# Score bursts of a causal attention block: two tiles in one bank, no splitting, and the mask written by VectorE

## The chip, the cores and the metric

One core of a Trainium2 chip runs the whole program. The metric is the device time of one execution in microseconds (us). The kernel before takes 1286.41 us as the median of three runs (1285.4 to 1286.81).

## The reference

Block-causal attention over 8 batches and 8 heads (576 positions, head size 64, blocks of 64 positions), followed by a two-layer network with a rational activation over all 4608 tokens:

```python
scores = scale * np.matmul(q, k.transpose(0, 1, 3, 2))          # 8 x 8 x 576 x 576
mask = (pos[:, None] // 64) >= (pos[None, :] // 64)
scores = np.where(mask, scores, -1000000000.0)
attn = softmax(scores)                                            # row maximum subtracted
x = (attn @ v) as 4608 x 512
h = x @ w_in                                                      # 512 -> 2048
g = (a0 + a1*h + a2*h^2 + a3*h^3) / (1 + |b0|*|h| + |b1|*h^2 + 1e-6)
out = g @ w_out                                                   # 2048 -> 512
```

## The kernel before

**Attention.** Heads are worked on in 32 pairs (`p` = 0 to 31, two heads each, called h = 0 and 1). `load` fetches q and k of a pair, `prep` transposes them on TensorE (PE) and splits each value into a rounded high part and a rest, so that a product is three matmul passes (high x high, high x low, low x high). A pair has five query tiles, taken in the order `TILES = (4, 3, 2, 0, 1)` (index `d`): tiles 0 to 3 are 128 query rows wide and see 128*(i+1) keys; tile 4 holds the last 64 rows of both heads and all 576 keys.

**Scores.** `scores(p, d, j)` emits the matmuls of one tile. For tiles 0 to 3 one head's contraction has only 64 rows, so head 0 uses the upper 64 rows of the PE array and head 1 the lower 64; matmuls of the two heads alternate, each head into a PSUM bank of its own, and `behind` keeps their order. In what follows such a group is called a burst, and its form shows in the profile as `64*128` (all other matmuls are `128*128`). In tiles 0 to 3 the last 64 keys of the first 64 rows are forbidden. Before, a matmul of the constant tiles `mrow` and `mcol` (line 504) adds -2^30 there, ahead of the three passes (line 507): two mask matmuls and six score matmuls per burst, in four bursts per pair.

**Softmax and the rest.** VectorE (DVE) reads each bank for the row maximum (line 518, tile `nm`), ScalarE (ACT) reads it for the exponential with its sum (`expo`, line 529), GpSimd (POOL) scales (line 541), PE transposes the probabilities (`transp`, line 567), ACT and DVE split them in high and low (580, 581), and PE multiplies with v (`pv`, lines 617 and 633). The results go through DRAM (`xscr`) to the network.

**The network.** Class `Ffn` works in units: `first` is the matmuls of line 210, then an activation spread over ACT, POOL and DVE, then `second` with the matmuls of line 277. Ten of sixteen column groups of the hidden layer are done while attention runs (phase 0), the other six after it (phase 1). Which unit is emitted beside which attention step is set by a table of due steps (`there`, `goal`).

**What sets the order.** Each engine works its own queue strictly in the order of the built program; waits between engines are semaphores. That order comes from a scheduler that runs the emitted program against its own model of times, honouring data dependencies and the extra edges made by `behind`. PSUM has 8 banks: five are the pool `ps_a` (tag `a`) of attention, from which scores, transposes and v products take one bank each in turn; one is `ps_h`, two are `ps_o`, of the network.

Of the kernel before, what the change touches and what calls it, by code (L numbers as in the profile page):

```python
# [8 lines left out]
F32 = mybir.dt.float32  # L9
F32R = mybir.dt.float32r  # L10
I32 = mybir.dt.int32
U32 = mybir.dt.uint32
AF = mybir.ActivationFunctionType
ALU = mybir.AluOpType
AX = mybir.AxisListType
# [10 lines left out]
LEND = 4  # L26
RL = 3
C0 = 0
RW = 4
EV = 6  # L30
DP = 12
# [24 lines left out]
NEG = -float(2 ** 30)  # L56
TILES = (4, 3, 2, 0, 1)
PH, PK = 30, 7
MASKS = ((None, None), (0, 0), (0, 1), (1, 0))
QC = 1.0 + 1e-6  # L60

WSCALE = 2.0 ** -112
# [3 lines left out]
def attn_ffn_kernel(  # L66
# [11 lines left out]
    nc = tc.nc  # L78
# [30 lines left out]
    class Weights:  # L109
# [22 lines left out]
        def convert(self):  # L132
            last = []
            for key in self.places:
# [8 lines left out]
                                        in_=src.bitcast(I32).rearrange("(d p) f -> p d f", p=128))  # L143
                if there and len(last) >= RW:
                    tc.add_manual_dep(got.ins, last[-RW].ins.name,
                                      mybir.DependencyInfo(mybir.DependencyClass.Sync, mybir.DependencyReason.DATA),
# [26 lines left out]
    class Ffn:  # L173
# [8 lines left out]
        def load(self, ph, c):  # L182
            n = CTS[ph]
            nd = 512 // n
            self.x[ph, c] = []
            for i in range(4 // nd):

                pool = self.pools[-1] if ph and (4 * c + i) % 6 < 3 else ffn
                x = pool.tile([128, nd, 2, n], F32R, name=f"x{ph}_{c}_{i}", tag="x", bufs=XB)
                t0 = c * n  # L190
                while t0 < (c + 1) * n:
                    b = t0 // S
                    t1 = min((c + 1) * n, (b + 1) * S)
                    for d in range(nd):
                        nc.sync.dma_start(out=x[:, d, :, t0 - c * n:t1 - c * n].bitcast(F32),
                                          in_=xscr[b][:, nd * i + d, :, t0 - b * S:t1 - b * S])
                    t0 = t1
                self.x[ph, c] += [x[:, d] for d in range(nd)]
# [135 lines left out]
    with ExitStack() as actx:  # L334
        ps_a = actx.enter_context(tc.tile_pool(name="ps_a", bufs=5, space=PSUM))
        att = actx.enter_context(tc.tile_pool(name="att", bufs=2))
        apers = actx.enter_context(tc.tile_pool(name="apers", bufs=1))
# [4 lines left out]
        pts.append(apers.tile([128, 640], F32, name="p4"))  # L342
        vz = apers.tile([128, 5, 2, 128], F32, name="vz", tag="v")
        vst = []
        mrow = apers.tile([128, 128], F32R, name="mrow")
        mcol = apers.tile([128, 64], F32R, name="mcol")
        for x in qtl:
            nc.gpsimd.memset(x.bitcast(F32), 0.0)
        nc.gpsimd.memset(mrow.bitcast(F32), 0.0)
        nc.gpsimd.memset(mcol.bitcast(F32), NEG)  # L350
        for r in (0, 64):
            nc.gpsimd.memset(mrow[r:r + 1, 0:64].bitcast(F32), 1.0)
        nc.gpsimd.memset(pts[4][:, S:], 0.0)
        nc.gpsimd.memset(vz, 0.0)

# [46 lines left out]
        def behind(ins, first):  # L402
            tc.add_manual_dep(ins.ins, first.ins.name,
                              mybir.DependencyInfo(mybir.DependencyClass.NoSync, mybir.DependencyReason.DATA),
                              reason="order")
# [74 lines left out]
        def scores(p, d, j):  # L480
            s = st_[p]
            if j == 0:
                s[d] = tuple(att.tile([128, 2], F32, name=f"{n}{p}_{d}", tag=n, bufs=4) for n in ("nm", "sm"))
            nm, sm = s[d]
            i = TILES[d]
            q, k = s["q"], s["k"]
            if i == 4:
                c0, w = 288 * j, 288
                ps = ps_a.tile([128, 512], F32, name=f"s{p}_{d}_{j}", tag="a")
                for n, (x, y) in enumerate(((0, 0), (0, 1), (1, 0))):  # L490
                    nc.tensor.matmul(ps[:, :w], lhsT=qtl[p % 2][:, x], rhs=k[:, y, c0:c0 + w],  # L491
                                     start=(n == 0), stop=(n == 2))
                s[d, j] = ps
            else:
                w = 128 * (i + 1)
                if j == 0:
                    for h in range(2):
                        s[d, h] = ps_a.tile([128, 512], F32, name=f"s{p}_{d}_{h}", tag="a")
                    prev = None
                    for n, (x, y) in enumerate(MASKS):  # L500
                        for h in (1, 0):
                            hs = slice(64 * h, 64 * h + 64)
                            if x is None:
                                mm = nc.tensor.matmul(s[d, h][:, w - 64:w], lhsT=mrow[hs], rhs=mcol[hs],  # L504
                                                      start=(n == 0), stop=(n == 3), skip_group_check=(n == 0))
                            else:
                                mm = nc.tensor.matmul(s[d, h][:, :w], lhsT=q[hs, x, 128 * i:128 * i + 128],  # L507
                                                      rhs=k[hs, y, 0:w], start=(n == 0), stop=(n == 3),
                                                      skip_group_check=(MASKS[0][0] is None))
                            if prev is not None:  # L510
                                behind(mm, prev)
                            prev = mm
            if i == 4 and j == 1:
                nc.vector.tensor_tensor_reduce(out=trash, in0=s[d, j][:, :w], in1=zero.to_broadcast([128, 288]),
                                               scale=-1.0, scalar=nm[:, 0:1], op0=ALU.add, op1=ALU.min,
                                               accum_out=nm[:, 0:1])
            else:
                nc.vector.reduce_max(out=nm[:, j:j + 1], in_=s[d, j][:, :w], axis=AX.X, negate=True)  # L518

        def expo(p, d, j):  # L520
            s = st_[p]
            nm, sm = s[d]
            i = TILES[d]
            if i == 4 and j == 0:
                return
            for j2 in (0, 1) if i == 4 else (j,):
                n, w = (0, 288) if i == 4 else (j2, 128 * (i + 1))
                dst = pts[4][:, 288 * j2:288 * j2 + 288] if i == 4 else pts[i][:, j2]
                nc.scalar.activation(out=dst, in_=s.pop((d, j2))[:, :w], func=AF.Exp,  # L529
                                     bias=nm[:, n:n + 1], scale=1.0, accum_out=sm[:, j2:j2 + 1])  # L530
            if j == 0:
                return
            rc = att.tile([128, 2], F32, name=f"rc{p}_{d}", tag="rc", bufs=4)
            n = 1 if i == 4 else 2
            if i == 4:
                nc.gpsimd.tensor_tensor(out=sm[:, 0:1], in0=sm[:, 0:1], in1=sm[:, 1:2], op=ALU.add)
            nc.gpsimd.tensor_scalar_add(rc[:, :n], sm[:, :n], 1e-9)
            nc.vector.reciprocal(rc[:, :n], rc[:, :n])  # L538
            for j2 in range(n):
                x = pts[4][:, 0:S] if i == 4 else pts[i][:, j2]  # L540
                nc.gpsimd.tensor_scalar(out=x, in0=x, scalar1=rc[:, j2:j2 + 1], scalar2=1.0,  # L541
                                        op0=ALU.mult, op1=ALU.mult)
# [102 lines left out]
        def attn_steps():  # L645
# [8 lines left out]
            for k in range(len(items) + ALAG2 + ALAG3 + 8):  # L654
                for x in [x for x in todo if x[0] == k]:
                    todo.remove(x)
                    x[1](*x[2])
                if k < len(items):
                    p, d, j = items[k]
                    if (d, j) == (0, 0):  # L660
                        if p + 1 < NV:
                            o0, o1, o2 = OFFS
                            at(k + o0, load, p + 1)
                            at(k + o1, prep, p + 1, 0)
                            at(k + o2, prep, p + 1, 1)
                    at(k + ALAG2, expo, p, d, j)
                    if j == 1:
                        at(k + TLAG, transp, p, d)
                        if d == 4:
                            at(k + TLAG + 1, pv, p, 0)  # L670
                            at(k + TLAG + 2, pv, p, 1)
                            if p + 1 < NV:
                                at(k + TLAG + 2, vprep, p + 1)
                    scores(p, d, j)
                yield k
# [4 lines left out]
        load(0)  # L680
        for _ in range(C0):
            next(wsteps)
# [18 lines left out]
        NWA, NWB = 2 * NFA, 2 * NFB  # L701
        wdone = C0
        WSTEPS = [0] * C0 + [(W0 * (i + 1)) // 4 for i in range(4 - C0)] + [WA + WD * i // 4 for i in range(NWA - 4)]

# [56 lines left out]
```

## Time and profile before

| what | value |
|---|---|
| median of three runs | 1286.41 us |
| profiled execution | 1287.04 us |
| its span, first to last instruction | 1285.3 us |
| granted PE clock | 0.998 of full |
| busy: PE, DVE, ACT, POOL | 1255.0, 904.0, 925.3, 880.5 us |
| mask matmuls (line 504) | 256, at 9.8 to 834.8 us |
| score matmuls (line 507) | 768, at 10.0 to 835.3 us |

Times are in us from the span's start. PE matmuls overlap each other, so the busy time of PE is more than what its matmuls stream; the distance from one matmul's start to the next one's start is what a matmul costs the queue. The last scores stand at 835 us: what comes after is the network alone.

### The profile page before, as it was taken

The numbers are of one execution on the slowest core, as the hardware profiler recorded it, in microseconds if no ns is written. First come the engines' busy times: TensorE is split into PE (matmuls) and PEld (weight loads), VectorE is DVE, ScalarE is ACT, GpSimd is POOL, SyncE is SP. The second block draws the span as 40 slices with busy tenths as digits, with TensorE's granted clock in tenths as the row PEclk, the third lists the DMA queues.
The fourth block names the chain that finished last, engine by engine and source line by source line (L and its number), as shares of the span: only waits on it lengthen the run. The fifth ranks groups of instructions, "written<-read, shape, count | busy, mean of one in ns | idle before, by whom it ended". The sixth has DMA issues, their size and how long they took to land.

```text
span 1285.3 us, 22748 instructions
## 1 busy us (share of the span) xinstructions
PE 1255.0 (98%) x7644; PEld 1059.5 (82%) x7644; DVE 904.0 (70%) x1703; ACT 925.3 (72%) x2047; POOL 880.5 (69%) x1041
## 2 busy tenths in 40 slices
PE   7989999999999999999999999999999999999997
PEld 5667888888888888888888888888998888888886
DVE  5767678777777777777767676754666767666675
ACT  5878777788678788777878787866766565555553
POOL 4656677777777878777767676766777666666564
PEclk9999999999999999999999999999999999999999
DMA  8772253445444354443432432356111433333423
GB/s 223 210 213 74 71 170 89 131 109 144 107 121 123 114 140 112 131 126 82 135 91 74 114 93 67 89 175 232 50 49 50 131 98 125 125 129 130 155 75 107
DMA packets 206516, 153.81 MB, mean 120 GB/s; under 512 B 137792, under 2 KB 170560, under 8 KB 206400
## 3 DMA queue, kind: packets, MB, share of 16 engines
q1 hardware_dynamic: 203920, 151.77, 40.5%
q8 instruction: 61, 1.00, 0.3%
q10 hardware_dynamic: 2416, 0.59, 0.2%
q14 instruction: 55, 0.45, 0.1%
q0 software_dynamic: 64, 0.00, 0.0%
HBM read 98.57 MB, written 44.04 MB: 111 GB/s over the span
## 4 chain that ended last, share of the span: by engine, by line
PE 82%; ACT 7%; DVE 4%; DMA 3%; POOL 3%; issue 1%; SPq 0%; ACTq 0%; POOLq 0%; DVEq 0%
PE h L210 30%; PE o L277 28%; PE o L633 6%; PE t L567 5%; PE s L507 4%; PE s L504 3%; ACT p L529 2%; PE tp L416 2%; PE s L491 1%; PE o L594 1%; DMA x<-xscr 1%; PE o L617 1%; DMA xscr<-xl 1%; POOL u L244 1%; ACT s L219 1%
## 5 line engine op out<-in xcount | busy, mean ns | idle before, releaser
L210 PE MATMUL h<-x,wpi 128*128 128x256 f32 (+1 forms) x2808 | 462.8, 312 | 3.1 <-DMA x<-xscr 1.7
L210 PEld LDWEIGHTS h<-x,wpi 128*128 128x128 f32 x2808 | 396.4, 190 | 40.6 <-issue 4.0
L277 PE MATMUL o<-wpo,gh 128*128 128x512 f32 x1152 | 351.0, 397 | 1.3 <-ACT os L287 1.3
L277 PEld LDWEIGHTS o<-wpo,gh 128*128 128x128 f32 x1152 | 211.1, 188 | 43.7 <-ACT os L287 1.8
L277 PE MATMUL o<-wpo,gl 128*128 128x512 f32 x576 | 213.8, 401 | 1.2 <-POOL gl L256 1.1
L224 POOL TENSOR_TENSOR u<-v,u 128x512 f32<-128x512 f32 x144 | 186.7, 1297 | 29.7 <-ACT v L220 24.6
L541 POOL TENSOR_SCALAR p<-p,rc 128x128 f32<-128x128 f32 (+4 forms) x288 | 169.2, 599 | 48.0 <-DVE rc L538 40.3
L529 ACT ACTIVATE p<-s,nm 128x288 f32<-128x288 f32 (+4 forms) x320 | 167.8, 533 | 45.1 <-DVE nm L518 39.9
L225 DVE TENSOR_TENSOR s<-s,h 128x512 f32<-128x512 f32 x144 | 98.4, 683 | 110.4 <-ACT s L219 56.7
L244 POOL TENSOR_TENSOR u<-s,u 128x512 f32<-128x512 f32 x90 | 116.7, 1297 | 72.1 <-DVE u L242 58.1
L232 ACT ACTIVATE v<-u,qcb 128x512 f32<-128x512 f32 x144 | 105.1, 730 | 74.7 <-POOL u L224 74.3
L217 ACT ACTIVATE u<-h 128x512 f32<-128x512 f32 x144 | 86.0, 597 | 93.7 <-PE h L210 87.9
L518 DVE TENSOR_REDUCE nm<-s 128x1 f32<-128x128 f32 (+4 forms) x288 | 128.5, 477 | 23.8 <-PE s L507 16.2
L567 PE MATMUL t<-ident,p 128*128 128x128 f32 x800 | 126.5, 281 | 0.9 <-POOL u L224 0.4
L581 DVE TENSOR_TENSOR ptrl<-t,ptrh 128x512 fp32r<-128x512 f32 (+1 forms) x182 | 111.6, 627 | 18.9 <-ACT ptrh L580 17.4
L277 PEld LDWEIGHTS o<-wpo,gl 128*128 128x128 f32 x576 | 104.3, 189 | 23.5 <-POOL gl L256 3.3
L256 POOL TENSOR_TENSOR gl<-u,v 128x512 fp32r<-128x512 f32 x90 | 118.6, 1317 | 3.4
L259 POOL TENSOR_TENSOR gl<-s,gh 128x512 fp32r<-128x512 f32 x54 | 69.9, 1294 | 62.9 <-ACT gh L258 62.9
L567 PEld LDWEIGHTS t<-ident,p 128*128 128x128 f32 x800 | 92.8, 142 | 23.1 <-issue 8.1
L580 ACT CAST ptrh<-t 128x512 fp32r<-128x512 f32 (+1 forms) x182 | 95.7, 545 | 18.8 <-PE t L567 18.2
L226 DVE SCALAR_TENSOR_TENSOR s<-s,coef,h 128x512 f32<-128x512 f32 x144 | 107.2, 744 | 2.9
L507 PE MATMUL s<-k,q 64*128 64x512 f32 (+3 forms) x768 | 103.5, 351 | 0.0
(109 smaller groups left out, 2105.6 us busy)
## 6 DMA issues: line engine op xcount, KB each, us to landing
x<-xscr SPq DMA_DIRECT2D x56, 256.0 KB, 3.8
xscr<-xl SPq DMA_DIRECT2D x32, 288.0 KB, 2.4
pscr<-os SPq DMA_DIRECT2D x18, 512.0 KB, 3.1
pt<-pscr SPq DMA_DIRECT2D x36, 256.0 KB, 4.3
out_dram<-os SPq DMA_DIRECT2D x36, 256.0 KB, 3.5
qr<-in_q_dram SPq DMA_DIRECT2D x64, 128.0 KB, 2.8
kr<-in_k_dram SPq DMA_DIRECT2D x62, 128.0 KB, 2.5
xt<-xh SPq DMA_DIRECT2D x52, 144.0 KB, 2.3
```

The source lines that it names most:

```text
L210: nc.tensor.matmul(h[:, j, :], lhsT=self.w[ph].win(f, dc, y), rhs=xs[dc][:, hl, :], start=(dc == 0 and i == 0), stop=(dc == 3 and i == 2))
L224: nc.gpsimd.tensor_tensor(out=ut, in0=vt, in1=ut, op=ALU.mult)
L226: nc.vector.scalar_tensor_tensor(out=st, in0=st, scalar=a1, in1=hf, op0=ALU.add if ph == 0 else ALU.subtract, op1=ALU.mult)
L244: nc.gpsimd.tensor_tensor(out=ut, in0=st, in1=ut, op=ALU.subtract)
L256: nc.gpsimd.tensor_tensor(out=gl, in0=ut, in1=vt, op=ALU.mult)
L277: nc.tensor.matmul(self.o[m], lhsT=g[:, j, ms], rhs=self.w[ph].wout(f, y), start=(u == 0 and j == 0 and i == 0), stop=(u == nu - 1 and j = ...
L507: mm = nc.tensor.matmul(s[d, h][:, :w], lhsT=q[hs, x, 128 * i:128 * i + 128], rhs=k[hs, y, 0:w], start=(n == 0), stop=(n == 3), skip_group ...
L518: nc.vector.reduce_max(out=nm[:, j:j + 1], in_=s[d, j][:, :w], axis=AX.X, negate=True)
L529: nc.scalar.activation(out=dst, in_=s.pop((d, j2))[:, :w], func=AF.Exp, bias=nm[:, n:n + 1], scale=1.0, accum_out=sm[:, j2:j2 + 1])
L541: nc.gpsimd.tensor_scalar(out=x, in0=x, scalar1=rc[:, j2:j2 + 1], scalar2=1.0, op0=ALU.mult, op1=ALU.mult)
L567: nc.tensor.transpose(ps[:, 128 * x:128 * x + 128], src[:, 128 * kb:128 * kb + 128], ident)
L581: nc.vector.tensor_tensor(out=dl, in0=src, in1=dh.bitcast(F32), op=ALU.subtract)
```

## The change

- The mask matmuls and their tiles `mrow` and `mcol` are gone. After a burst, VectorE writes -2^30 over the forbidden 64 x 64 block of each head's bank (a memset, line 515 of the changed kernel), and the row maximum follows it.
- Tiles 2 and 0 share a burst: head h has one bank with tile 2 in columns 0 to 383 and tile 0 in columns 384 to 511. The burst has 12 matmuls. A pair has three bursts instead of four and takes six score banks instead of eight for tiles 0 to 3.
- Ahead of each burst VectorE writes one column of head 0's bank (a memset of 128 x 1, line 498), and the burst's first matmul, which is head 1's, waits for that (`held`). So a burst starts only when both banks are free. `TP = 0` applies this to all pairs.

```diff
-MASKS = ((None, None), (0, 0), (0, 1), (1, 0))
+PASSES = ((0, 0), (0, 1), (1, 0))
...
-        mrow = apers.tile([128, 128], F32R, name="mrow")
-        mcol = apers.tile([128, 64], F32R, name="mcol")
...
-        nc.gpsimd.memset(mrow.bitcast(F32), 0.0)
-        nc.gpsimd.memset(mcol.bitcast(F32), NEG)
-        for r in (0, 64):
-            nc.gpsimd.memset(mrow[r:r + 1, 0:64].bitcast(F32), 1.0)
...
-                if j == 0:
+                if j == 0 and i:
+                    both = [ps_a.tile([128, 512], F32, name=f"s{p}_{d}_{h}", tag="a") for h in range(2)]
+                    parts = ((2, 0), (0, 384)) if i == 2 else ((i, 0),)
+                    for t, c in parts:
+                        for h in range(2):
+                            s["s", t, h] = both[h][:, c:c + 128 * (t + 1)]
+                    prev = None
+                    held = nc.vector.memset(both[0][:, 0:1], 0.0) if p >= TP else None
+                    for n, (x, y) in enumerate(PASSES):
+                        for t, c in parts:
+                            for h in (1, 0):
+                                hs = slice(64 * h, 64 * h + 64)
+                                mm = nc.tensor.matmul(s["s", t, h], lhsT=q[hs, x, 128 * t:128 * t + 128],
+                                                      rhs=k[hs, y, 0:128 * (t + 1)], start=(n == 0 and t == i),
+                                                      stop=(n == 2), skip_group_check=True)
+                                if prev is not None:
+                                    behind(mm, prev)
+                                elif held is not None:
+                                    tc.add_manual_dep(mm.ins, held.ins.name,
+                                                      mybir.DependencyInfo(mybir.DependencyClass.Sync, mybir.DependencyReason.DATA),
+                                                      reason="order")
+                                prev = mm
                     for h in range(2):
...
-                            if x is None:
-                                mm = nc.tensor.matmul(s[d, h][:, w - 64:w], lhsT=mrow[hs], rhs=mcol[hs],
-                                                      start=(n == 0), stop=(n == 3), skip_group_check=(n == 0))
...
+                        m = both[h].rearrange("p (s t) -> p s t", t=64)[0:64, 2 * i + 1:8:2][:, :len(parts)]
+                        nc.vector.memset(m, NEG)
...
-                nc.vector.reduce_max(out=nm[:, j:j + 1], in_=s[d, j][:, :w], axis=AX.X, negate=True)
+                nc.vector.reduce_max(out=nm[:, j:j + 1], in_=s[d, j][:, :w] if i == 4 else s["s", i, j],
+                                     axis=AX.X, negate=True)
```

The scheduler makes a new order from this. On the whole of PE, the built program before has its 1024 mask and score matmuls in 201 stretches without another matmul between: 55 whole bursts of eight, and 73 bursts of which the first mask matmul stands alone, apart from the other seven. The changed one has 96 stretches, 64 of six and 32 of twelve. On DVE, 288 memsets come in: 96 of 128 x 1, 128 of 64 x 64 and 64 of 64 x 2 x 64.

On PE before, this is the place around 403 us of the trace, the burst of tile 0 (`s_3_1` and `s_3_0` are its banks of heads 1 and 0; the second number in a bank's name is `d`):

```order
L633 MATMUL o_0_5544<-ptrl,vst 128x64
L504 MATMUL s_3_1_5568<-mcol,mrow 128x64 [waits Activation_49]
L210 MATMUL h_5_0_5613<-x_5_0_5428,wpi_0_0_346 128x256 [waits DVE_49]
L210 MATMUL h_5_0_5613<-x_5_0_5428,wpi_0_0_346 128x256 x5
L504 MATMUL s_3_0_5567<-mcol,mrow 128x64 [waits DVE_49]
L507 MATMUL s_3_1_5568<-k_5034,q_5033 128x128
L507 MATMUL s_3_0_5567<-k_5034,q_5033 128x128
```

The first mask matmul stands by itself between matmuls of the other form. After the change tile 0 is in the burst of tile 2 (banks `s_2_1` and `s_2_0`; here the place in the same network unit, `h_5_0`):

```order
L211 MATMUL h_5_0_5589<-x_5_1_5410,wpi_0_2_541 128x256
L503 MATMUL s_2_1_5033<-k_4590,q_4589 128x384 [waits Activation_49]
L503 MATMUL s_2_0_5032<-k_4590,q_4589 128x384 [waits PE_49]
L503 MATMUL s_2_1_5033<-k_4590,q_4589 128x128
L503 MATMUL s_2_0_5032<-k_4590,q_4589 128x128
...
L211 MATMUL h_5_0_5589<-x_5_1_5410,wpi_0_2_541 128x256 x3
```

All twelve score matmuls stand together (the dots leave out the other two passes). On DVE before, tiles 2 and 0 of one pair (`nm_2` and `nm_3` are the row maxima of tile 2 and tile 0):

```order
L518 TENSOR_REDUCE nm_2_5475<-s_2_1_5478 128x1 [waits PE_49]
L518 TENSOR_REDUCE nm_2_5475<-s_2_0_5477 128x1 [waits PE_49]
...
L636 TENSOR_TENSOR xl_5534<-o_0_5544,xh_5533 64x512 [waits Activation_49]
L518 TENSOR_REDUCE nm_3_5565<-s_3_1_5568 128x1 [waits PE_49]
L518 TENSOR_REDUCE nm_3_5565<-s_3_0_5567 128x1 [waits PE_49]
```

On DVE after the change, the same two tiles of a pair:

```order
L498 MEMSET s_2_0_5032 128x1 [waits DVE_49]
L521 TENSOR_REDUCE nm_1_4957<-s_1_1_4960 128x1 [waits DVE_49]
...
L394 SCALAR_TENSOR_TENSOR q_5013<-tp_0_5015,q_5013 128x512 [waits Activation_49]
L515 MEMSET s_2_1_5033 64x2x64 [waits PE_49]
L515 MEMSET s_2_0_5032 64x2x64 [waits PE_49]
L521 TENSOR_REDUCE nm_2_5030<-s_2_1_5033 128x1 [waits DVE_49]
L521 TENSOR_REDUCE nm_2_5030<-s_2_0_5032 128x1 [waits DVE_49]
L585 TENSOR_TENSOR ptrl<-t_4_0_5070,ptrh 128x2x2x128 [waits Activation_49]
L521 TENSOR_REDUCE nm_3_5141<-s_2_1_5033 128x1 [waits Activation_49]
L394 SCALAR_TENSOR_TENSOR k_5014<-tp_1_5077,k_5014 128x512 [waits Activation_49]
L521 TENSOR_REDUCE nm_3_5141<-s_2_0_5032 128x1 [waits Activation_49]
```

The column memset of the coming burst stands nine rows ahead of the burst's mask memsets, the mask memsets wait for PE and the reductions of tile 2 for them, and the reductions of tile 0, which waited for PE before, now wait for ACT.

More of the change, by code (lines that the diff above doesn't have):

```diff
@@ L28 @@
 C0 = 0
+TP = 0
 RW = 4
@@ L495, in scores @@
                 w = 128 * (i + 1)
-                if j == 0:
-                    for h in range(2):
[L498 to L502, printed above, removed]
-                            if x is None:
-                                mm = nc.tensor.matmul(s[d, h][:, w - 64:w], lhsT=mrow[hs], rhs=mcol[hs],
-                                                      start=(n == 0), stop=(n == 3), skip_group_check=(n == 0))
[L506 to L512, printed above, removed]
+                if j == 0 and i:
[20 more added lines that the diff above has]
+                                prev = mm
+                    for h in range(2):
+                        m = both[h].rearrange("p (s t) -> p s t", t=64)[0:64, 2 * i + 1:8:2][:, :len(parts)]
+                        nc.vector.memset(m, NEG)
@@ L528, in expo @@
                 dst = pts[4][:, 288 * j2:288 * j2 + 288] if i == 4 else pts[i][:, j2]
-                nc.scalar.activation(out=dst, in_=s.pop((d, j2))[:, :w], func=AF.Exp,
+                nc.scalar.activation(out=dst, in_=s.pop((d, j2))[:, :w] if i == 4 else s.pop(("s", i, j2)), func=AF.Exp,
                                      bias=nm[:, n:n + 1], scale=1.0, accum_out=sm[:, j2:j2 + 1])
```

## The prediction

> **What bounds the kernel now.** First the page: busy shares, and below them the chain of work that ended last, by engine.
>
> ```profile
> PE 1255.0 (98%) x7644; PEld 1059.5 (82%) x7644; DVE 904.0 (70%) x1703; ACT 925.3 (72%) x2047; POOL 880.5 (69%) x1041
> ...
> PE 82%; ACT 7%; DVE 4%; DMA 3%; POOL 3%; issue 1%; SPq 0%; ACTq 0%; POOLq 0%; DVEq 0%
> ```
>
> PE is busy for 98% of the span, and 82% of the chain is PE. Since a share over the whole span mixes stages, next comes the table of windows: before 150 us, from there to the last scores, and after them. Its columns are stretch, length, then busy us and count for PE, PE's weight loads, DVE, ACT and POOL, then clock and DMA.
>
> ```profile
> 0.00:150.00 150.00, 135.73 (x813) 102.57 (x813) 103.90 (x245) 110.72 (x304) 86.80 (x158) 1.00 0.59 163
> 150.00:835.00 685.00, 678.32 (x4614) 582.33 (x4613) 507.45 (x1042) 544.51 (x1305) 510.43 (x642) 1.00 0.41 112
> 835.00:1286.00 451.00, 440.95 (x2222) 374.65 (x2220) 292.64 (x418) 270.07 (x439) 283.28 (x243) 1.00 0.35 117
> ```
>
> From 150 to 835 us PE is busy for 678.3 of 685 us, DVE for 507.5 (74%), ACT for 544.5 (79%) and POOL for 510.4 (75%). In the first 150 us PE has gaps (135.7 of 150). After 835 us no scores are left, and the change touches nothing there. The chain inside the first two stretches, by line:
>
> ```profile
> by line: PE h L210 23.8%; PE o L277 22.3%; PE o L633 10.6%; PE t L567 8.0%; PE s L507 6.4%; PE s L504 4.5%; PE tp L416 2.5%; PE s L491 1.9%; ACT p L529 1.8%; PE o L617 1.3%; POOL u L244 0.9%; issue 0.9%; ACT ptrh L580 0.9%; ACT s L219 0.8%;
> ```
>
> ```profile
> by line: PE o L594 11.4%; ACT p L529 5.9%; DMA xscr<-xl 5.3%; PE t L567 5.3%; PE h L210 5.1%; issue 4.8%; PE s L507 4.6%; DMA coef<-in_moe_b_dram 3.0%; DMA qr<-in_q_dram 3.0%; ACT pt L578 2.9%; PE s L491 2.8%; PE tp L416 2.7%; DMA kr<-in_k_
> ```
>
> In the long stretch the PE entries listed (23.8, 22.3, 10.6, 8.0, 6.4, 4.5, 2.5, 1.9 and 1.3) make 81.3%; mask matmuls (line 504) alone hold 4.5% of 685 us, 31 us, for a 64-column product. In the first stretch the listed PE entries make 31.9%: there other engines and DMA decide as often. So what PE saves is worth about 0.81 of itself in the one and 0.32 in the other.
>
> What a mask matmul costs the queue is read from the timeline of PE, from start to start. Columns: start, length, operation, tiles, shape, count.
>
> ```profile
> 395.56 0.30 PE L504 MATMUL s<-mcol,mrow 64*128 64x64 f32 x2
> 395.69 0.77 PE L507 MATMUL s<-k,q 64*128 64x384 f32 x6
> 396.40 0.66 PE L567 MATMUL t<-ident,p 128*128 128x128 f32 x4
> ...
> 402.73 0.28 PE L633 MATMUL o<-ptrl,vst 128*128 128x64 f32 x1
> 402.94 0.29 PE L504 MATMUL s<-mcol,mrow 64*128 64x64 f32 x1
> 403.16 0.97 PE L210 MATMUL h<-x,wpi 128*128 128x256 f32 x6
> 404.06 0.29 PE L504 MATMUL s<-mcol,mrow 64*128 64x64 f32 x1
> 404.06 0.66 PE L507 MATMUL s<-k,q 64*128 64x128 f32 x6
> 404.65 0.51 PE L633 MATMUL o<-ptrh,vst 128*128 128x512 f32 x1
> ...
> 406.18 0.28 PE L633 MATMUL o<-ptrl,vst 128*128 128x64 f32 x1
> 406.29 0.65 PE L567 MATMUL t<-ident,p 128*128 128x128 f32 x4
> ...
> 409.13 0.30 PE L504 MATMUL s<-mcol,mrow 64*128 64x64 f32 x2
> 409.26 0.60 PE L507 MATMUL s<-k,q 64*128 64x256 f32 x6
> 409.79 0.73 PE L277 MATMUL o<-wpo,gh 128*128 128x512 f32 x2
> ```
>
> The lone mask matmul at 402.94 starts 0.21 us after the 64-wide product of line 633, and the next matmul starts 0.22 us later: from 402.73 to 403.16 are 0.43 us. The same 64-wide product is followed in 0.11 us where no burst intervenes (406.18 to 406.29). One lone mask costs 0.43 - 0.11 = 0.32 us, though it streams 64 columns. A pair of masks at the head of a whole burst costs 0.13 us (409.13 to 409.26).
>
> **The change part by part.** The sum is made against the profiled execution, 1287.04 us (span 1285.3 and 1.7 around it), which lies 0.6 us above the median of the runs, 1286.41.
>
> *Lone masks.* The order before has 73 of them, after none: 73 x 0.32 = 23.4 us of PE.
>
> *Mask pairs.* In whole bursts scores take 0.53 us at 256 columns (409.26 to 409.79) and 0.71 at 384 (395.69 to 396.40), 0.18 more for 128 columns. Tile 0's scores should then take 0.35, and its split burst takes 0.59 from the second mask on (404.06 to 404.65), so the second mask isn't free there either. I count the pair's 0.13 us for each of the 128 bursts: 16.6 us.
>
> *Merged tiles.* Tile 0's burst is 0.59 - 0.13 = 0.46 us without masks. Inside the burst of tile 2 its matmuls should cost what 128 more columns cost, 0.18. Saved 0.28 us, 32 times: 9.0 us.
>
> Together 49.0 us of PE queue time. Where it lies, by the masks of line 504 in the two windows:
>
> ```profile
> 0.00:150.00 150.00, 13.84 (x59) 8.90 (x59) 1.00 0.59 163
> 150.00:835.00 685.00, 48.07 (x197) 30.07 (x197) 1.00 0.41 112
> ```
>
> 197 of 256, 77%, fall in the stretch that PE bounds: 37.7 us there, 11.3 in the first 150. With the PE shares of the two chains: 37.7 x 0.81 + 11.3 x 0.32 = 34.2 us off the end.
>
> A rule speaks here. The masks stream 64 columns, and by the row at 402.94 one costs 0.32 us when alone. The Trainium skill, TensorEngine Tiling (Array Packing), Instruction Overhead, says that a matmul has about 60 cycles of overhead whatever its width; 256 masks of 64 cycles at the 2.4 GHz of TensorE: Matmul & The Clock Gate would be 7 us, an estimate from the two pages, and with the merged tiles the queue time would be 16 us in place of 49. The same page's Key Properties says that changing the tiling mode drains the engine, which agrees with the 0.21 and 0.22 us on both sides of the lone mask. The sum goes by the rows.
>
> *Memsets on VectorE.* 288 are added, and the trace has one, to another memory:
>
> ```profile
> L102 DVE MEMSET qcb<- x1: 59/59/59, 0.8 to 0.8; 128x1 f32 x1
> ```
>
> Other rows bound it: small operations that read or write PSUM, and what ACT does to the same banks.
>
> ```profile
> L529 ACT ACTIVATION_READ_ACCUMULATOR p<-s,nm 128x1 f32 x320 | 68.4, 214 | 0.0
> L529 ACT ACTIVATE p<-s,nm 128x384 f32<-128x384 f32 x64 | 38.2, 608 | 0.8 <-DVE nm L518 0.8
> L226 DVE SCALAR_TENSOR_TENSOR s<-s,coef,h 128x512 f32<-128x512 f32 x144 | 107.2, 744 | 2.9
> L624 DVE TENSOR_TENSOR xl<-o,xh 64x64 f32<-64x64 f32 x52 | 11.4, 218 | 4.1 <-ACT xh L621 3.7
> L538 DVE RECIPROCAL rc<-rc 128x2 f32<-128x2 f32 x128 | 20.8, 162 | 66.0 <-POOL rc L537 64.4
> L518 DVE TENSOR_REDUCE nm<-s 128x1 f32<-128x128 f32 x64 | 15.8, 279 | 3.2 <-PE s L507 3.0
> ```
>
> A 128 x 1 memset lies between 59 ns and the 162 ns of a reciprocal; I take 70, near the only memset. A 64 x 64 block lies between 59 and the 218 ns of line 624, which also reads PSUM; I take 130. A 64 x 2 x 64 lies between 59 and the 279 of a 128-wide reduction; I take 200. Per pair 3 x 0.07 + 4 x 0.13 + 2 x 0.20 = 1.13 us, 36 in all (bounds 17 and 61). DVE is idle for 178 us of the long stretch, which covers its 28; without that cover the rivals below apply. What is not covered is order: two memsets stand between a burst and its row maximum. ACT waits for that maximum in 29 places:
>
> ```profile
> ACT p L529 <- DVE nm L518: 35.1, 29, 3.5
> PEld s L504 <- issue: 9.4, 36, 0.6
> PEld s L504 <- ACT p L529: 4.0, 7, 1.7
> ```
>
> There 0.26 to 0.40 us comes on top, and about half of it counts because other work is ready: 29 x 0.3 x 0.5 = 4 us.
>
> *The column memset.* It comes between a bank's last reader and the burst, in DVE's queue, and PE's whole queue stands behind the burst. Before, 43 of 197 masks (36 and 7 in the two rows of waits on line 504) found PE idle. The same share of 96 bursts is 21; each then waits for the memset (0.07) and on average for half of an operation ahead of it, 0.744 us on line 226: 21 x 0.44 = 9 us. Bounds: nothing, where DVE comes early, and 96 x 0.74 = 71 us. I take the low value since the order sets this memset nine rows ahead of the burst's end.
>
> *Banks and start.* Two banks less per pair are asked for, but tile 0's half holds its bank until tile 2 is read too; I put the two against each other at nothing, with the 21 bursts above as the cover that would go. Four memsets leave POOL's start; PE's first transposes wait for a transfer at that time, so this is nothing:
>
> ```profile
> 4.41 1.08 PE L416 MATMUL tp<-ident,qr 128*128 128x128 f32 x4 [4.41 <-DMA qr<-in_q_dram]
> ```
>
> Sum: 34.2 - 4 - 9 = 21 us; 1287 - 21 = 1266.
>
> **The rivals.**
>
> *Masks only fill time that PE would wait anyway.* A scheduler puts a lone mask ahead because the second bank is not free. If the 23.4 us turn into waiting, 25.6 are left: 25.6 x (0.77 x 0.81 + 0.23 x 0.32) - 13 = 5 us, 1282. For it: the 43 idle places. Against: the rows around 402.94 show no idle time ahead of the mask or behind it. The Trainium skill's overhead rule, weighed above, ends near this case: 7 us of masks at most would put the time at 1280 even without deductions.
>
> *Another engine becomes the bound.* With 30 us off the stretch ACT is at 544.5 of 655 (83%) and DVE at 535.5 (82%), in queues that wait for each other. If PE's share of the chain falls from 0.81 to 0.4, 37.7 x 0.4 + 3.6 - 13 = 6 us are left: 1281. Against: three engines at under 80% let PE be busy for 99% now.
>
> *The shared bank.* In the new order the row maximum of tile 0 waits for ACT, where it waited for PE: two exponentials of tile 2, 2 x (0.608 + 0.214) = 1.64 us per pair in which DVE's queue can stand, 52 us in all. If 0.66 us per pair reaches PE, the 21 us are gone and the time is 1287. Against: other DVE work stands between the two reductions and their predecessors. The Trainium skill, PSUM — Partial Sum Buffer, PSUM bank collisions raise a hardware error, asks for two engines to be kept apart on one bank and quadrant even where both read; the new wait agrees with it, and the trace before has no shared bank to show its price.
>
> *PE waits for the column memset, and the kernel gets slower.* Without the 9 us the gain is 30; 30 / 96 = 0.31 us per burst is the point from which it decides. One DVE operation of 0.744 us ahead of the memset that is late at two bursts of three gives 0.5 us: 48 - 30 = 18 us slower, 1305. For it: a single queue now releases every burst, and DVE will be fuller. Against: DVE idles a quarter of the stretch, and before the change its own results are late for ACT in 29 places only.
>
> **How the numbers follow.** The forecast case, 1253 to 1279, has 0.56: its ends are the sum without the two deductions, 1287 - 34, and with both doubled, 1287 - 8. More of the 49 us reaching the end, down to 1238, has 0.07. Masks as filling 0.08, another bound 0.10: all these are faster. The shared bank eating the gain has 0.07 and is the case of no change; waiting for the column memset has 0.12 and is slower. A change of under 0.2% (2.6 us) can't be told from none here. So faster 0.81, same 0.07, slower 0.12. The range 1243 to 1284 holds the forecast, most of the two weak gains and part of the full one, about 0.78.
>
> **What the profile after would show.** Right: no `64*128` matmul of 64 columns, 96 bursts, score matmuls followed by the next form without a second start; PE's busy time in the attention stage down by some 45 us; the last scores near 810 to 815 us; DVE memsets of 60 to 200 ns, some 36 us in all; few waits of the bursts for DVE. Wrong in the price: bursts that still show 0.3 us of gaps on both sides, or memsets over 220 ns. Wrong in the cover: PE waits for the column memset (line 498) over 0.3 us per burst, or DVE's reductions of tile 0 wait for ACT for over 0.6 us per pair, and the chain's share of PE before 815 us under 0.6. What would make it wrong as a whole is an order in which the network's matmuls, which fill PE now, come out later than they are needed.

## The result and the profile after

The changed kernel takes 1269.24 us as a median (1268.14 to 1272.39), against 1285.95 for the kernel before on the same chip: a ratio of 0.9873, 95% interval 0.9854 to 0.9893. The profiled execution took 1268.71 us with a span of 1266.9, 18.4 less than before. The forecast was 1266, between 1243 and 1284.

The page after, its busy shares and its chain by engine:

```profile
PE 1206.9 (95%) x7388; PEld 1027.8 (81%) x7388; DVE 927.4 (73%) x1991; ACT 922.9 (73%) x2047; POOL 890.5 (70%) x1037
...
PE 60%; ACT 13%; POOL 12%; DVE 9%; issue 4%; DMA 2%; SPq 0%; ACTq 0%; POOLq 0%; DVEq 0%
```

PE's busy time fell by 48.1 us (1255.0 to 1206.9), the span by 18.4. The rest, 29.7 us, is time in which PE now stands idle: span less PE's busy time is 60.0 us, and was 30.3. PE's share of the chain fell from 82% to 60%.

The same three stretches (length, then busy us of PE, its weight loads, DVE, ACT and POOL):

```profile
0.00:150.00 150.00, 128.35 (x769) 96.79 (x770) 109.56 (x309) 112.68 (x304) 90.45 (x155) 0.97 0.58 163
150.00:835.00 685.00, 662.23 (x4568) 578.77 (x4567) 538.03 (x1290) 559.67 (x1336) 529.76 (x657) 1.00 0.42 115
835.00:1267.00 432.00, 416.34 (x2055) 352.23 (x2053) 279.82 (x395) 250.54 (x407) 270.33 (x226) 0.99 0.35 117
```

From 150 to 835 us, PE idles 22.8 us of 685 where it idled 6.7, in the first 150 us 21.7 (before 14.3). The chain inside the long stretch, by line:

```profile
by line: PE h L211 18.4%; PE o L278 16.4%; PE o L637 8.6%; PE t L571 5.5%; PE s L503 5.0%; issue 3.6%; POOL gl L257 2.9%; ACT p L533 2.9%; POOL p L545 2.4%; POOL u L245 2.0%; POOL u L225 1.9%; POOL xl L644 1.9%; PE tp L411 1.7%; DVE u L243 
```

The PE entries shown make 55.6% (18.4, 16.4, 8.6, 5.5, 5.0, 1.7); 81.3% stood there before. Both lists are cut off at the end of the line. POOL's lines hold 2.9, 2.4, 2.0, 1.9 and 1.9% now, where one with 0.9% was listed before. The timeline of PE near 400 us shows both the gain and where it went:

```profile
397.76 0.63 PE L571 MATMUL t<-ident,p 128*128 128x128 f32 x4 [0.93 <-DVE ptrl L585]
...
400.38 0.73 PE L278 MATMUL o<-wpo,gl 128*128 128x512 f32 x2 [0.92 <-POOL gl L257]
...
402.33 2.43 PE L211 MATMUL h<-x,wpi 128*128 128x256 f32 x19
404.70 1.07 PE L503 MATMUL s<-k,q 64*128 64x384 f32 x12
405.70 0.66 PE L571 MATMUL t<-ident,p 128*128 128x128 f32 x4
...
416.43 0.62 PE L503 MATMUL s<-k,q 64*128 64x256 f32 x6
416.98 1.10 PE L211 MATMUL h<-x,wpi 128*128 128x256 f32 x7
```

The merged burst takes 1.00 us from start to next start (404.70 to 405.70), and the burst of tile 1 takes 0.55 (416.43 to 416.98), where 409.13 to 409.79 were 0.66. But the network's second layer (line 278) waited 0.92 us for POOL ahead of 400.38, and a transpose 0.93 ahead of 397.76.

The memsets on DVE (mean ns behind the busy us):

```profile
L515 DVE MEMSET s<- 64x64 f32 x128 | 12.2, 112 | 9.2 <-PE s L503 8.7
...
L515 DVE MEMSET s<- 64x128 f32 x64 | 9.8, 165 | 2.1 <-PE s L503 1.6
...
L498 DVE MEMSET s<- 128x1 f32 x96 | 5.7, 59 | 4.1 <-ACT p L533 2.9
```

59, 112 and 165 ns; 27.7 us in all.

### The profile page after: what moved, and what is told of

The parts are those of the page before. It is cut to its first block, busy times and chain, and to the rows that moved or that the text cites. A ratio compares the mean times of both kernels' runs of the same rounds, so it can differ in the third digit from the quotient of the medians.

```text
span 1266.9 us, 22540 instructions
## 1 busy us (share of the span) xinstructions
PE 1206.9 (95%) x7388; PEld 1027.8 (81%) x7388; DVE 927.4 (73%) x1991; ACT 922.9 (73%) x2047; POOL 890.5 (70%) x1037
## 4 chain that ended last, share of the span: by engine, by line
PE 60%; ACT 13%; POOL 12%; DVE 9%; issue 4%; DMA 2%; SPq 0%; ACTq 0%; POOLq 0%; DVEq 0%
PE h L211 22%; PE o L278 22%; PE o L637 5%; PE t L571 3%; PE s L503 3%; ACT p L533 3%; POOL gl L257 3%; POOL u L245 3%; POOL u L225 2%; POOL p L545 2%; PE o L598 1%; DVE nm L521 1%; DVE gh L242 1%; ACT v L233 1%; ACT u L218 1%
## 5 line engine op out<-in xcount | busy, mean ns | idle before, releaser
L278 PE MATMUL o<-wpo,gh 128*128 128x512 f32 x1152 | 347.3, 396 | 3.0 <-ACT os L288 2.0
L278 PE MATMUL o<-wpo,gl 128*128 128x512 f32 x576 | 211.1, 401 | 7.4 <-POOL gl L257 7.3
L225 POOL TENSOR_TENSOR u<-v,u 128x512 f32<-128x512 f32 x144 | 190.9, 1326 | 33.7 <-ACT v L221 28.9
L545 POOL TENSOR_SCALAR p<-p,rc 128x128 f32<-128x128 f32 (+4 forms) x288 | 172.9, 611 | 46.2 <-DVE rc L542 35.3
L226 DVE TENSOR_TENSOR s<-s,h 128x512 f32<-128x512 f32 x144 | 98.4, 684 | 102.4 <-ACT s L220 55.3
L571 PE MATMUL t<-ident,p 128*128 128x128 f32 x800 | 121.8, 279 | 9.0 <-POOL p L545 3.6
L278 PEld LDWEIGHTS o<-wpo,gl 128*128 128x128 f32 x576 | 104.6, 190 | 30.3 <-POOL gl L257 11.0
L242 DVE TENSOR_TENSOR gh<-s,v 128x512 fp32r<-128x512 f32 x90 | 74.7, 830 | 35.8 <-ACT v L240 34.8
```

Of the source, the lines that this page charges most:

```text
L225: nc.gpsimd.tensor_tensor(out=ut, in0=vt, in1=ut, op=ALU.mult)
L278: nc.tensor.matmul(self.o[m], lhsT=g[:, j, ms], rhs=self.w[ph].wout(f, y), start=(u == 0 and j == 0 and i == 0), stop=(u == nu - 1 and j = ...
L571: nc.tensor.transpose(ps[:, 128 * x:128 * x + 128], src[:, 128 * kb:128 * kb + 128], ident)
```

## The experiments

Idle is the span less PE's busy time, both from the page of the profiled run; stretches are runs of score (and mask) matmuls on PE in the built order. The run's ratio is to the kernel before on the same chip, with its 95% interval. The two profiles of the changed kernel differ by 4.9 us in PE's busy time and by 3.6 us in idle time, so differences of that size between rows say nothing. Every variant gets an order of its own from the scheduler.

| kernel | stretches | PE busy | idle | median us | ratio |
|---|---|---|---|---|---|
| before | 201 | 1255.0 | 30.3 | 1285.95 | 1 |
| changed | 96 | 1206.9 | 60.0 | 1269.24 | 0.9873 (0.9854 to 0.9893) |
| changed, again | 96 | 1211.8 | 56.4 | 1268.12 | 0.9856 (0.9837 to 0.9876) |
| e1: no hold | 165 | 1246.5 | 48.8 | 1294.38 | 1.0059 (1.0039 to 1.0078) |
| e2: hold alone | 127 | 1228.0 | 52.3 | 1282.29 | 0.9970 (0.9958 to 0.9983) |
| e3: no merge | 127 | 1217.4 | 53.6 | 1273.41 | 0.9896 (0.9879 to 0.9913) |
| e4: masks on PE | 96 | 1218.0 | 46.8 | 1266.60 | 0.9843 (0.9825 to 0.9860) |
| e5: memsets twice | 96 | 1206.9 | 63.2 | 1274.38 | 0.9910 (0.9889 to 0.9930) |
| e6: no mask | 96 | 1205.3 | 61.4 | 1269.15 | 0.9863 (0.9842 to 0.9883) |
| e7: mixed masks | 96 | 1211.8 | 50.6 | 1265.13 | 0.9832 (0.9811 to 0.9853) |
| f1: changed, no scaling | 96 | 1203.3 | 46.8 | 1252.23 | 0.9737 (0.9723 to 0.9750) |
| f2: before, no scaling | 206 | 1262.5 | 37.0 | 1301.20 | 1.0117 (1.0103 to 1.0131) |
| f3: changed, no bias | 96 | 1207.1 | 55.3 | 1266.06 | 0.9847 (0.9834 to 0.9861) |
| f4: before, no bias | 196 | 1251.1 | 33.7 | 1287.23 | 1.0019 (1.0008 to 1.0030) |

**e1, without the hold.**

```diff
-TP = 0
+TP = 99
```

> The changed kernel without the column memset and the wait on it; its order has 165 stretches of score matmuls in place of 96, with some 70 split bursts again. Theory (PE's queue is what counts, at about 0.38 of its price, as 18 of 49 us came through): 70 x 0.3 = 21 us of PE come back, 8 us of them at the end, about 1277. Rival (the wait on VectorE's column memset causes the new PE waits): those waits go too, and the time is at or under the changed kernel's 1269.

It is slower than the kernel before. PE's busy time is 39.6 us above the changed kernel's, twice what was expected for 70 splits. The timeline of PE in this run shows why:

```profile
442.33 0.71 PE L211 MATMUL h<-x,wpi 128*128 128x256 f32 x4
442.98 0.44 PE L503 MATMUL s<-k,q 64*128 64x384 f32 x1
443.35 0.74 PE L211 MATMUL h<-x,wpi 128*128 128x256 f32 x4
444.02 1.07 PE L503 MATMUL s<-k,q 64*128 64x384 f32 x11
445.02 0.66 PE L571 MATMUL t<-ident,p 128*128 128x128 f32 x4
...
462.11 2.30 PE L211 MATMUL h<-x,wpi 128*128 128x256 f32 x18
464.34 0.50 PE L503 MATMUL s<-k,q 64*128 64x512 f32 x1
464.77 0.74 PE L211 MATMUL h<-x,wpi 128*128 128x256 f32 x4
```

The piece that stands alone is now a score matmul of 384 or 512 columns, not a mask of 64. It takes 0.37 us (442.98 to 443.35) and 0.43 (464.34 to 464.77) to the next start, against 0.22 for a lone mask, and streams without its partner of the other head. The burst after it is no shorter for that: its 11 matmuls take 1.00 us (444.02 to 445.02), as all 12 do in the changed kernel. The step into the lone piece costs as well: up to its start, four matmuls of line 211 take 0.65 us and eighteen take 2.23, which makes 0.11 us for each and 0.20 for the step. A split then costs 0.57 to 0.63 us (an estimate from these rows), and the 69 stretches more make 39 to 43; 39.6 were measured. Both expectations missed the time: the theory of PE's queue holds with a price twice as high, and the rival is refuted, since with the wait gone the time rises by 25 us. Without mask matmuls the hold carries the whole gain: without it the kernel is 8 us slower than the one before.

**e2, the hold alone.**

```diff
+                    held = nc.vector.memset(s[d, 0][:, 0:1], 0.0)
                     prev = None
...
+                            else:
+                                tc.add_manual_dep(mm.ins, held.ins.name, ...)
```

> The kernel before with the column memset and the wait alone; masks stay PE matmuls, four bursts per pair, none split. Theory: 73 lone masks at 0.32 us = 23 us of PE saved, some 9 us at the end: 1277. Rival (the hold costs what it saves): 1286 or more.

PE's busy time falls by 27.0 us (23 expected) and the span by 5.0; idle time takes the other 22. The median lies between the theory's 1277 and the rival's 1286. A good part of the new idle time is waits of the bursts for their banks. These are all rows in which PE waits ahead of a mask (line 505 here), with total us, times and longest:

```profile
PE s L505 <- ACT p L534: 5.0, 7, 1.5
...
PE s L505 <- DVE ptrl L586: 3.5, 2, 2.2
PE s L505 <- ACT pt L583: 3.2, 3, 1.5
...
PE s L505 <- DVE s L499: 1.6, 2, 1.1
...
PE s L505 <- ACT q L396: 1.3, 1, 1.3
PE s L505 <- DVE xl L607: 1.2, 1, 1.2
```

They make 15.8 us; the masks of the kernel before waited 3.7 us (rows further below).

**e3, no merge.**

```diff
-                if j == 0 and i:
+                if j == 0:
...
-                    parts = ((2, 0), (0, 384)) if i == 2 else ((i, 0),)
+                    parts = ((i, 0),)
```

> The changed kernel with tile 0 in a burst and banks of its own again; hold and VectorE masks stay. Theory: 9 us of PE come back, 3 at the end: about 1272. Rival (the shared bank delays the softmax of tile 0 and holds banks longer): faster than the changed kernel, 1263 or less.

1273.4, as the theory has it: PE's busy time rises by 10.5 us (9.0 expected) and the time by about 4. With banks of their own for tiles 2 and 0 the kernel isn't faster, so a cost of the shared bank doesn't show.

**e4, masks on PE.** Two mask matmuls per tile at the head of the pass loop of each burst, no block memsets:

```diff
-PASSES = ((0, 0), (0, 1), (1, 0))
+PASSES = ((None, None), (0, 0), (0, 1), (1, 0))
...
+                                if x is None:
+                                    mm = nc.tensor.matmul(s["s", t, h][:, 128 * t + 64:128 * t + 128], lhsT=mrow[hs],
+                                                          rhs=mcol[hs], start=(t == i), stop=False, skip_group_check=True)
...
-                        nc.vector.memset(m, NEG)
```

> Merged and unsplit bursts as in the changed kernel, but the mask is added by PE matmuls at the head of each burst, and VectorE has only the column memset. Theory: PE pays 96 x 0.13 = 12 us again, 5 at the end: about 1274. Rival (VectorE's 192 block memsets on the way to the row maximum cause the new waits): faster than the changed kernel, 1263 or less.

1266.6, between the two expectations and slightly under the changed kernel, with intervals that overlap. From its page:

```profile
span 1264.8 us, 22855 instructions
...
PE 1218.0 (96%) x7644; PEld 1042.8 (82%) x7644; DVE 910.2 (72%) x1799; ACT 925.0 (73%) x2047; POOL 883.1 (70%) x1041
```

PE is busy for 11.1 us more and idle for 13.2 us less. So with merged bursts, to move the mask from PE to VectorE bought nothing that can be measured. With four bursts per pair it did, as e2 to e4 and the changed kernel show side by side (all with the hold; median us, and PE's busy us behind it):

| | masks on PE | masks on VectorE |
|---|---|---|
| four bursts | e2: 1282.3 (1228.0) | e3: 1273.4 (1217.4) |
| three, merged | e4: 1266.6 (1218.0) | changed: 1269.2 (1206.9) |

PE's busy time adds up: the masks are worth 10.6 and 11.1 us, the merge 10.0 and 10.5. The time doesn't: the move of the masks is worth 8.9 us with four bursts and nothing with merged ones, the merge 15.7 us with masks on PE and 4.2 with masks on VectorE. What of a saving on PE reaches the end can't be given for each part by itself.

In the merged form this could mean that the memsets are a price, or that time saved on PE is no longer worth anything; e6 and e5 are to tell these apart.

**e6, no mask at all.**

```diff
-                    for h in range(2):
-                        m = both[h].rearrange("p (s t) -> p s t", t=64)[0:64, 2 * i + 1:8:2][:, :len(parts)]
-                        nc.vector.memset(m, NEG)
```

> The changed kernel with the 192 block memsets left out, so the forbidden blocks aren't masked at all; the column memsets and the merged, unsplit bursts stay, and PE's queue is that of the changed kernel. Theory (the block memsets between burst and row maximum cause the waits that the PE-masked form doesn't have, some 17 us): about 1252. Rival (PE's queue being shorter, the other engines set the pace, whatever the memsets do): 1266 to 1269.

Span and busy shares from its page:

```profile
span 1266.7 us, 22316 instructions
...
PE 1205.3 (95%) x7388; PEld 1028.8 (81%) x7388; DVE 908.9 (72%) x1799; ACT 924.5 (73%) x2047; POOL 887.4 (70%) x1037
```

1269.15, as the changed kernel beside it (1268.12). The block memsets cost nothing that shows, although VectorE is busy for 18.5 us less; idle stays at 61.4 us. The time is the rival's. That the other engines set the pace now is its explanation and isn't shown by this run.

**e5, memsets twice.**

```diff
                         nc.vector.memset(m, NEG)
+                        nc.vector.memset(m, NEG)
```

> The changed kernel with each of the 192 block memsets done twice in a row, some 25 us more of VectorE. Theory (the memsets stand on the path): as much again as they cost, about 1284. Rival (they are covered): within 3 us of the changed kernel.

6 us slower than the changed kernel beside it, for 18 us more of VectorE's busy time (927.4 to 945.4). Neither expectation: one set of memsets is covered, and a second isn't wholly. A worse order could do the same; the runs don't separate the two.

**e7, mixed masks.** From e4: PE masks tiles 3 and 1, VectorE the merged burst.

```diff
+                        if x is None and i == 2:
+                            continue
...
+                    if i == 2:
+                        for h in range(2):
+                            m = both[h].rearrange("p (s t) -> p s t", t=64)[0:64, 5:8:2]
+                            nc.vector.memset(m, NEG)
```

> Merged and unsplit bursts; VectorE masks the merged burst alone (64 memsets), PE masks tiles 3 and 1. Theory: a third of the memsets' waits, 6 us, against 4 to 6 us of PE saved to the form with all masks on PE: 1265 to 1268, no better. Rival (a memset that serves two tiles is worth it): 1262 or less.

1265.13, as the theory has it, the fastest here that computes the whole reference, and 3 us under the changed kernel beside it; the two intervals overlap.

**The changed kernel again**, beside e5 to e7, unchanged:

> The changed kernel again, on the chip of the three beside it, for comparison: 1269.

1268.12, where the first runs had 1269.24.

**f1 to f4, whose queue sets the pace.** f1 and f2 leave out POOL's scaling, in the changed kernel and in the one before; f3 and f4 leave out one activation of the network.

```diff
-            for j2 in range(n):
-                x = pts[4][:, 0:S] if i == 4 else pts[i][:, j2]
-                nc.gpsimd.tensor_scalar(out=x, in0=x, scalar1=rc[:, j2:j2 + 1], scalar2=1.0,
-                                        op0=ALU.mult, op1=ALU.mult)
```

> The changed kernel without the scaling of the probabilities on GpSimd (line 545: 288 operations, 173 us of POOL), so the output isn't normalised; PE's queue is the same. Theory (POOL and the softmax chain through it set the pace once PE's queue is 49 us shorter): the new waits of PE, some 30 us, go: 1250 or less. Rival (ScalarE's queue does): 1264 or more.

> The kernel before without the same scaling, as control. Theory: PE is the bound there, with 38 us of waits of which half lie in the first 150 us: 1276 to 1286, so that the change, beside this, is worth more than the 18 us it brought: 30 or more. Rival: the same difference of 18 us as with the scaling.

```diff
-                nc.scalar.activation(out=st, in_=st, func=AF.Identity, bias=a0)
```

> The changed kernel without one activation in place per network unit of phase 0 on ScalarE (90 operations of 0.74 us, 66 us of ACT), which adds the constant a0, so the output lacks that term; PE's queue is the same. Theory (POOL sets the pace): 1264 or more. Rival (ScalarE's queue sets it): 1250 or less.

> The kernel before without the same activation, as control. Theory and rival: PE is the bound there, 1280 to 1286; if ScalarE sets the changed kernel's pace, the difference to it grows from 18 us to 30 or more.

With POOL relieved by 173 us (890.5 to 717.7), the changed kernel falls to 1252.23, just above the theory's 1250 and far from the rival's 1264, and its idle time from 60.0 to 46.8 us; the PE entries in its chain from 150 to 835 us are back at 73.9% (24.2, 20.2, 10.9, 7.0, 6.8, 2.1, 1.5, 1.2):

```profile
by line: PE h L211 24.2%; PE o L278 20.2%; PE o L633 10.9%; PE t L567 7.0%; PE s L503 6.8%; ACT p L533 2.5%; issue 2.5%; PE tp L411 2.1%; PE s L486 1.5%; POOL u L245 1.3%; POOL gl L257 1.3%; PE o L617 1.2%; DVE nm L521 1.2%; DMA x<-xscr 1.1
```

With ACT relieved by 50 us (922.9 to 873.0), it falls by 2 to 3 us (f3). The control f4 takes 1287.23, a little over the 1280 to 1286 expected, so the difference between the two is 21 us and not the 30 that ScalarE's rival asks for: ScalarE's queue isn't the limit. VectorE, relieved by 18.5 us in e6, gave nothing. That leaves POOL's queue, or the scaling as a step of the softmax between the exponential and the transposes; f1 takes away both at once and can't tell them apart.

Nor is it settled that it is either. The control f2 (1276 to 1286 expected) became slower by 15 us, with 7.5 us more on PE (79 lone masks instead of 73, among others) and 6.7 more idle, though work was only taken away. Each kernel gets a new order from the scheduler, and this pair shows that the order can move the time by as much as the effect looked for. So f1's 17 us may be a better order, in part or in whole, and the difference of 49 us between f2 and f1 isn't read as the worth of the change.

## Why the prediction was right

**The price on PE's queue** was the carrying step, and its sum held: 49.0 us by starts of matmuls, 48.1 measured as busy time. Its parts held less well. From the kernel before over e2 and e3 to the changed one, the lone masks are worth 27.0 us (23.4 forecast), the mask pairs 10.6 (16.6 forecast) and the merge 10.5 (9.0 forecast). A pair at the head of a burst thus cost 0.08 us (10.6 / 128), not the 0.13 from start to start. That the errors cancel to within 1 us is luck, since two profiles of one kernel differ by 4.9. The overhead rule of the Trainium skill (TensorEngine Tiling (Array Packing), Instruction Overhead), 7 us for all masks, is far below the 27.0 us that the lone masks alone were worth. That changing the tiling mode drains TensorE, as the same page of the Trainium skill says under Key Properties, fits the price of a lone mask.

**How much comes through** was forecast as 21 of 49 us, and 18.4 came. The size was right and the account behind it partly wrong. The sum took off 28 us: 15 for the chain's share on other engines, 4 for the memsets and 9 for the column memset. Measured, 29.7 us became idle time of PE; the waits of PE that the trace lists, all rows summed, grew from 23.2 to 52.1 us.

- The memsets: 27.7 us of VectorE against 36 estimated, and no time that shows (e6).
- The column memset: the trace puts 1.0 us of PE's waits down to it in three places, not 9 us. The row stands under the waits for line 498 in the changed kernel:

```profile
L498 DVE MEMSET s<- x96: 59/59/59, 9.6 to 822.8; 128x1 f32 x96
...
  PE s L503: 1.0, 3
```

- The hold itself: the bursts together waited 3.7 us before and wait 12.0 now (the rows of lines 504 and 503 below), 8.3 more. The 9 us came true, but as waits for the last readers of the two banks on ACT (`p`) and DVE (`ptrl`). The hold is what brings them: every run here that has it shows 5.6 to 15.8 us of such waits, and the four without it (before, e1, f2, f4) 3.3 to 4.5. The count of 21 bursts behind the 9 us was also read from the wrong rows: those of line 504 that begin with PEld are waits of weight loads, and the same view has PE itself waiting ahead of line 504 in three places. That 9 and 8.3 agree is luck.
- The chain's share: this step was mis-sized. The old share of PE, 0.81, was applied as if it stayed; the PE entries listed fell to 0.56 with the change. The waits of PE other than those of the bursts grew by 20.6 us, where the step had put 15. The rival "another engine becomes the bound" named ACT and VectorE; POOL has a part as well. Before:

```profile
PE s L504 <- ACT p L529: 2.3, 4, 1.2
...
PE o L277 <- POOL gl L256: 1.1, 3, 0.8
...
PE s L504 <- ACT pt L578: 0.9, 1, 0.9
...
PE s L504 <- DVE ptrl L581: 0.5, 1, 0.5
```

After:

```profile
PE o L278 <- POOL gl L257: 7.3, 8, 1.4
PE s L503 <- ACT p L533: 5.8, 8, 1.5
...
PE s L503 <- DVE ptrl L585: 3.8, 3, 2.0
PE t L571 <- POOL p L545: 3.6, 4, 1.6
...
PE s L503 <- DVE s L515: 1.4, 1, 1.4
...
PE s L503 <- DVE s L498: 1.0, 3, 0.4
```

The second layer's wait for POOL's `gl` grew from 1.1 to 7.3 us, and transposes wait for POOL's scaled probabilities (`p`) for 3.6. Over all rows, PE's waits that POOL ended grew from 1.5 to 11.2 us, those that DVE ended from 3.3 to 18.1, and those that ACT ended from 11.5 to 15.9: no single engine took over.

Why PE idles more stays open in part. A shorter queue on PE isn't needed for it: without the hold (e1) PE is busy for 1246.5 us, nearly as before, and idles for 48.8 against 30.3. The order before has the least idle time of all in the table. That the table of due steps, which no run changes, suits that order better than the new ones would explain part of the loss; this is untested.

**The rivals.** "Masks only fill waiting time" is borne out in part: in e2 the lone masks are gone, 22 of their 27 us became idle time, and the bursts' waits rose from 3.7 to 15.8 us; the 1282.3 there is near the 1282 that this rival forecast for the whole change. It fails for the changed kernel, where with the merge and the masks on VectorE 18.4 us came through. "The shared bank" isn't borne out: e3 is no faster, and DVE idles ahead of all its row maxima for ACT for 3.3 us in ten places, 0.10 us per pair, against the 0.66 at which the gain would be gone:

```profile
L521 DVE TENSOR_REDUCE nm<-s x288: 220/450/693, 10.9 to 830.2; 128x1 f32<-128x512 f32 x32, 128x1 f32<-128x384 f32 x32, 128x1 f32<-128x128 f32 x32, 128x1 f32<-128x256 f32 x32
...
  ACT p L533: 3.3, 10
```

"PE waits for the column memset" is refuted by e1 and the row of line 498 above. The forecast named last scores near 810 to 815 us as a sign; the last burst starts at 827.7, only some 7 us earlier than before. PE used the time that it saved mostly for the network: up to 835.3 us the trace has 1682 matmuls of its first layer (line 211), where the one before has 1600, and 828 of the second, where it has 768.

## What to carry over

Count the changes of form on a saturated PE queue, not only the columns: a lone 64-column matmul cost 0.32 us, and a split that left a score matmul alone some 0.6 (an estimate). A rule that holds a group until all its banks are free has a price too, in waits for the banks: with merged bursts it was worth 25 us of time, by itself 4. Then ask how long the engine stays the bound: a saving of 48 us on PE met 30 us of new idle time, and with merged bursts moving the masks off PE was worth nothing more. A control without the change can be disturbed by a new order as much as the kernel under study; one order per variant is no measurement of an engine's worth.

## What the runs showed of the hardware

At some places the granted clock of PE halves for some 3.4 us after a wait. One place in the changed kernel, windows first (the clock is the third column from the end), then the timeline of PE:

```profile
640.00:650.00 10.00, 8.61 (x64) 7.45 (x62) 8.52 (x19) 8.81 (x19) 9.05 (x9) 1.00 0.46 132
650.00:654.00 4.00, 4.00 (x22) 3.69 (x19) 3.00 (x9) 3.27 (x10) 2.54 (x7) 0.58 0.14 55
654.00:660.00 6.00, 6.00 (x46) 5.09 (x45) 4.17 (x10) 4.11 (x8) 5.11 (x5) 1.00 0.19 44
```

```profile
647.11 0.64 PE L486 MATMUL s<-k,qtl 128*128 128x288 f32 x3
649.13 0.36 PE L211 MATMUL h<-x,wpi 128*128 128x256 f32 x1 [1.39 <-DVE rc L542]
649.42 0.96 PE L503 MATMUL s<-k,q 64*128 64x512 f32 x6
650.31 4.27 PE L211 MATMUL h<-x,wpi 128*128 128x256 f32 x21
654.42 0.60 PE L571 MATMUL t<-ident,p 128*128 128x128 f32 x4
```

A mean clock of 0.58 over 4 us is half the clock for 3.4 us (0.42 x 4 / 0.5). After a wait of 1.39 us, one matmul and a burst, 21 matmuls took 4.1 us to the next start, 0.20 each; 19 of the same form took 2.37 us at 402.33 (to 404.70), 0.125 each. So this place cost 1.5 us.

A wait of this length doesn't always bring it. Before, a wait of 1.24 us ahead of 422.41 brought no such window. In the second profile of the changed kernel the clock is 0.57 from 352 to 356 us, after a wait of 1.59 us; in the first, after a wait of 2.03 us at the same place, it is 1.00 (351 to 355). What decides it, these runs don't show.

The first profile of the changed kernel has six such windows ahead of the end, the kernel before one, and the second profile of the changed kernel nine; there PE is busy for 4.9 us longer. The mean clock of a run was 0.989 to 0.999 for the kernel before and 0.985 to 0.991 for the changed one. The time lost this way stands in PE's busy time, not in its idle time, so at an equal clock PE's busy time would have fallen by more than 48.1 us.
